# Fourier filter and cosine gate on one core: shared places for gate tiles, an earlier second batch, and unread products in two of TensorE's waits

## The chip, the cores and the metric

One core of one Trainium2 chip runs the kernel. The time is device microseconds of one execution; of the kernel before there are three runs, 2515.46, 2516.33 and 2518.54 us, median 2516.33. A profile of one further execution, taken by the hardware profiler, is read throughout.

## The reference

```python
# x: (8, 3008, 256); filters: (1505, 256); w_in: (256, 2048); w_out: (2048, 256), float32
X = np.fft.rfft(x, axis=1)
y = np.fft.irfft(X * (filt_r + 1j * filt_i)[None], n=3008, axis=1)
y = y.reshape(8 * 3008, 256)
h = y @ w_in
g = h * np.cos(h)
return g @ w_out
```

Every sequence is filtered in the frequency domain, and then each of the 24064 tokens goes through a hidden layer of 2048 with the gate h cos(h).

## The kernel before, in words

**The transforms.** 3008 is 47 x 64, so a sequence's transform is done as two short ones, written as matrix products: `stage1` (length 47; 7 pieces a batch), `stage23` (length 64, the filter, and length 64 back; 12 pieces a batch) and `stage4` (length 47 back; units of up to five short sequences, which give the columns of `y`). Between the stages the data goes through HBM: ScalarE's queue writes `z1t` and `z2t`, SyncE's queue (SP) reads `xf`, `zf`, `f` and `z` (`z4` in the code). Batch 0 has code of its own (`first1`, `first23`), whose products are plain float32; the others split each float32 number into a high and a low part (`xh`, `xl`; `zh`, `zl`; `yh`, `yl`) and add three products (`mm3`).

**The hidden layer.** The tokens come in 47 chunks of 512 (`c`), the hidden units in 8 parts of 256 (`s`), so there are 376 steps. `hidden(c, s)` makes `hp` with 12 products of 128x128 by 128x512 (L469), and `gate` turns it into `gh` and `gl`: two VectorE operations bring h into the range of the sine (L481, L482), ScalarE takes the sine (L483), VectorE multiplies by h (L484), ScalarE casts the high part `gh` (L485), and GpSimd subtracts it to leave the low part `gl` (L486). `project(c, s)` adds three products of `gh` and `gl` with `w_out` into `acc` (L497), two steps later (`LAG = 2`). After the eighth part ScalarE writes `acc` to the tile `o` (L514) and a transfer takes it out. `hp` has two places in PSUM, `acc` one for each half. So the products of step k+2 need L484 of step k to have read `hp`.

**Places.** A tile's name or tag has a number of places, and a new tile waits until an old one's last reader is done. `g`, `gh`, `gl` have two each of 4 KB a partition, `o` two of 2 KB; the transforms' results `z1t` and `z2t` share the tag `st` with four places of 2 KB.

**Order.** The 376 steps are written one behind the other, 8 slots each. A planner (`plan`, `run_due`) gives each part of a transform a due slot and hands it out between the parts of the steps, TensorE's parts at least `APART = 3` slots apart. Batch b is planned to end at slot 376 b - `BEFORE`; batch 1 gets `LATER` slots more, and starts at `FIRST`. A unit of `stage4` is handed out when all of its batch's `stage23` pieces have been written. From all this a scheduler with a timing model writes each engine's order of instructions at compile time; `tc.high_priority()` puts instructions ahead there, `tc.issue_after(i)` puts them behind `i` on its engine. At run time every engine follows its own order. The weights are split into high and low parts by `prep_w` while the first steps run (L231 to L239, on ScalarE, VectorE and GpSimd).

The places and the plan before, the lines that the change touches:

```python
LATER = 54
...
g = moe.tile([P, 2, TC], F32, name="g")
gs[c, s] = gh, gl = [moe.tile([P, 2, TC], F32R, name=v) for v in ("gh", "gl")]
...
o = moe.tile([P, TC], F32, name="o")
...
end = slot(b * S) - BEFORE
if b == 1:
    end += LATER
start = max(end - LENGTH, FIRST)
step = (end - start - GAP12) / (2 * n1 + 2 * n23)
```

## Time and profile before

| what | value |
|---|---|
| median of three runs | 2516.33 us |
| profiled execution, whole | 2517.33 us |
| its span, first to last instruction | 2515.5 us |
| mean granted TensorE clock | 0.988 |
| TensorE busy | 2454.9 us (98%) |
| VectorE busy | 1889.6 us (75%) |
| GpSimd busy | 1426.9 us (57%) |
| ScalarE busy | 1286.4 us (51%) |

Busy time is time in which an engine has an instruction under way; products overlap at their ends. PE is TensorE's products, PEld its weight loads, DVE is VectorE, ACT is ScalarE, POOL is GpSimd, SP is SyncE, and a q behind an engine's name is its queue of instructions. A row of the timeline gives the start, the length, the engine, the line of the kernel, the operation, what it writes and reads, how many instructions are merged, and in brackets how long the engine had been idle and what ended that. The granted clock is the share of full speed that TensorE's throttle allowed.

### The profile page before, as it was taken

To read this page: it belongs to the slowest core of one execution; us is meant where nothing else is said; L and a number is where in the kernel's file an instruction comes from. 1 tells how busy PE (TensorE), PEld (TensorE's weight loads), DVE (VectorE), ACT (ScalarE), POOL (GpSimd) and SP (SyncE) were. 2 spreads that over 40 slices of the span, in tenths; PEclk is the share of its full clock that TensorE was granted. 3 is DMA by queue.
4 is the path that set the end of the run, shared out by engine and by line. 5 is a ranking of instruction groups with operands and counts; after the bars stand their busy time and mean duration, and the time that the engine had idled before them with its cause. 6 is when DMAs were issued, how large, how long until landed. Compare 5 with 4: busy or idle time off the path is not lost.

```text
span 2515.5 us, 29899 instructions
## 1 busy us (share of the span) xinstructions
PE 2454.9 (98%) x10783; PEld 1967.7 (78%) x10783; DVE 1889.6 (75%) x1917; ACT 1286.4 (51%) x1709; POOL 1426.9 (57%) x825
## 2 busy tenths in 40 slices
PE   7789999999999999999999999999999999999999
PEld 2567777888888888888888888888888888888887
DVE  2697886887678876888678877788768886666666
ACT  1654555555455554555545555555555554444443
POOL 1775665656556655656556565565656654444443
PEclk8799999999999999999999999999999999999999
DMA  9633334223232221322223232222313211000000
GB/s 321 208 91 96 120 105 129 91 79 91 70 93 90 96 79 51 108 88 87 79 76 100 85 110 61 82 96 75 89 40 98 96 47 49 30 17 9 17 9 18
DMA packets 135121, 212.27 MB, mean 84 GB/s; under 512 B 12765, under 2 KB 64781, under 8 KB 134973
## 3 DMA queue, kind: packets, MB, share of 16 engines
q1 hardware_dynamic: 82577, 137.85, 18.4%
q10 hardware_dynamic: 52396, 72.50, 8.8%
q8 instruction: 86, 1.41, 0.2%
q14 instruction: 62, 0.51, 0.1%
HBM read 135.33 MB, written 74.97 MB: 84 GB/s over the span
## 4 chain that ended last, share of the span: by engine, by line
PE 85%; DVE 7%; DMA 3%; issue 2%; ACT 2%; POOL 1%; SPq 0%; ACTq 0%; DVEq 0%; POOLq 0%
PE hp L469 38%; PE acc L497 37%; PE ps L435 3%; PE ps L251 2%; PE ps L252 2%; PE ps L253 2%; DVE g L481 1%; DVE sw L325 1%; DVE g L482 1%; DVE g L484 1%; DMA xf<-in_x 1%; ACT g L483 1%; DVE xo L280 1%; DMA zf<-z 0%; PE hp L378 0%
## 5 line engine op out<-in xcount | busy, mean ns | idle before, releaser
L486 POOL TENSOR_TENSOR gl<-g,gh 128x1024 fp32r<-128x1024 f32 x375 | 908.6, 2423 | 812.8 <-ACT gh L485 490.9
L469 PE MATMUL hp<-y,w_in 128*128 128x512 f32 x4512 | 1138.8, 401 | 18.4 <-DVE g L484 15.9
L469 PEld LDWEIGHTS hp<-y,w_in 128*128 128x128 f32 x4512 | 846.2, 190 | 219.0 <-issue 9.4
L497 PE MATMUL acc<-gh,w_out 128*128 128x512 f32 x3008 | 896.2, 396 | 1.3 <-ACT gh L485 1.3
L484 DVE TENSOR_TENSOR g<-g,hp 128x1024 f32<-128x1024 f32 x377 | 458.1, 1215 | 326.6 <-ACT g L483 325.6
L483 ACT ACTIVATE g<-g,half_pi 128x1024 f32<-128x1024 f32 x377 | 433.6, 1150 | 479.9 <-DVE g L482 435.4
L497 PEld LDWEIGHTS acc<-gh,w_out 128*128 128x128 f32 x3008 | 563.1, 188 | 132.2 <-ACT gh L485 2.2
L485 ACT CAST gh<-g 128x1024 fp32r<-128x1024 f32 x377 | 395.2, 1048 | 401.5 <-DVE g L484 381.9
L481 DVE TENSOR_SCALAR g<-hp 128x1024 f32<-128x1024 f32 x377 | 458.6, 1216 | 126.3 <-PE hp L469 122.0
L497 PE MATMUL acc<-gl,w_out 128*128 128x512 f32 x1504 | 548.3, 399 | 0.1
L482 DVE SCALAR_TENSOR_TENSOR g<-g,hp 128x1024 f32<-128x1024 f32 x377 | 457.9, 1215 | 9.4
L497 PEld LDWEIGHTS acc<-gl,w_out 128*128 128x128 f32 x1504 | 282.8, 188 | 65.1 <-POOL gl L486 0.7
L435 PEld LDWEIGHTS ps<-m,z 120*128 120x128 f32 (+1 forms) x816 | 129.3, 193 | 29.2 <-DMA z<-z 7.8
L452 POOL TENSOR_TENSOR y<-y,y 128x470 fp32r<-128x470 f32 (+29 forms) x142 | 127.1, 899 | 42.9 <-ACT y L449 42.8
L331 POOL TENSOR_TENSOR yl<-ya,yh 128x512 fp32r<-128x512 f32 x84 | 111.5, 1328 | 58.2 <-ACT yh L330 55.7
L314 POOL TENSOR_TENSOR zl<-zf,zh 128x512 fp32r<-128x512 f32 x84 | 111.9, 1333 | 48.2 <-DVE zh L313 21.1
L435 PE MATMUL ps<-m,z 120*128 120x120 f32 (+1 forms) x816 | 130.4, 275 | 7.5 <-DMA z<-z 7.0
L325 DVE SCALAR_TENSOR_TENSOR sw<-sw,sg,f 128x256 f32<-128x256 f32 x168 | 116.7, 734 | 0.0
L330 ACT CAST yh<-ya 128x512 fp32r<-128x512 f32 x84 | 51.8, 618 | 115.1 <-DVE ya L327 115.1
L313 DVE CAST zh<-zf 128x512 fp32r<-128x512 f32 x84 | 86.2, 1026 | 29.8 <-DMA zf<-z 18.2
L327 DVE TENSOR_TENSOR ya<-ya,sw 128x512 f32<-128x512 f32 x84 | 100.6, 1198 | 0.1
L280 DVE TENSOR_TENSOR xo<-xf 120x512 f32<-120x512 f32 (+1 forms) x49 | 55.0, 1123 | 40.9 <-DMA xf<-in_x 40.8
(98 smaller groups left out, 1429.2 us busy)
## 6 DMA issues: line engine op xcount, KB each, us to landing
z<-z SPq DMA_DIRECT2D x101, 240.0 KB, 3.2
out_t<-o ACTq DMA_DIRECT2D x93, 256.0 KB, 2.0
f<-in_fb SPq DMA_DIRECT2D x84, 256.0 KB, 3.1
f<-in_fa SPq DMA_DIRECT2D x84, 256.0 KB, 3.4
zf<-z SPq DMA_DIRECT2D x84, 256.0 KB, 3.5
z<-z2t ACTq DMA_DIRECT2D x84, 256.0 KB, 2.0
xf<-in_x SPq DMA_DIRECT2D x42, 480.0 KB, 4.3
z<-z1t ACTq DMA_DIRECT2D x84, 240.0 KB, 2.5
```

Source lines behind the costliest of these rows:

```text
L314: nc.gpsimd.tensor_tensor(lo, zf, hi.bitcast(F32), ALU.subtract)
L325: nc.vector.scalar_tensor_tensor(sw[:, ks], sw[:, ks], sg[:, 2 * i + k : 2 * i + k + 1], fbt[:, ks], ALU.mult, ALU.mult)
L435: nc.tensor.matmul(v[:, t, a * r : (a + 1) * r], zf[:, a, t * P : (t + 1) * P], mats[f"m4{a}"][:r, :r], start=True, stop=True)
L452: (nc.vector if i < 2 * n_first else nc.gpsimd).tensor_tensor(yl, part, yh.bitcast(F32), ALU.subtract)
L469: nc.tensor.matmul(hp[:, u], w_in[s][w][:, t, fs], y[:, t], start=(t == 0 and n == 0), stop=(t == NDT - 1 and n == 2))
L481: nc.vector.tensor_scalar(g, h, 0.25, MAGIC, ALU.add, ALU.add)
L482: nc.vector.scalar_tensor_tensor(g, g, MAGIC, h, ALU.subtract, ALU.subtract)
L483: nc.scalar.activation(g, g, AF.Sin, bias=half_pi, scale=-TWO_PI)
L484: nc.vector.tensor_tensor(g, g, h, ALU.mult)
L485: nc.scalar.copy(gh, g)
L486: engine.tensor_tensor(gl, g, gh.bitcast(F32), ALU.subtract)
L497: nc.tensor.matmul(acc, w_out[s][w][:, u, es], g[:, u], start=(s == 0 and u == 0 and n == 0), stop=(s == NFT // 2 - 1 and u == 1 and n == 2))
```

## The change

Five edits. The last piece of `first23` (batch 0) gets six products that nobody reads behind its last product (`WARM4`), and step (0, 1) gets sixteen behind its last (`WARM_GATE`); both write a place of `acc`. `g` and `gl` share one tag with five places instead of two and two. `o` takes its place among the four of `st`. `LATER` is 44 instead of 54.

```diff
-LATER = 54
+LATER = 44
...
+WARM4, WARM_GATE = 6, 16
...
+    def keep_busy(after, m, data, times):
+        with tc.issue_after(after), tc.high_priority():
+            ps = ps_o.tile([P, 512], F32, name="acc0")
+            for _ in range(times):
+                nc.tensor.matmul(ps[: m.shape[1], : data.shape[1]], m, data, start=True, stop=True)
...
-            nc.tensor.matmul(ps, mats["f3i"], yb, start=False, stop=True)
+            m = nc.tensor.matmul(ps, mats["f3i"], yb, start=False, stop=True)
+            if i == n23 - 1:
+                keep_busy(m.ins, mats["f3i"], yb, WARM4)
...
-        g = moe.tile([P, 2, TC], F32, name="g")
-        gs[c, s] = gh, gl = [moe.tile([P, 2, TC], F32R, name=v) for v in ("gh", "gl")]
+        g = moe.tile([P, 2, TC], F32, name="g", tag="g", bufs=5)
+        gh = moe.tile([P, 2, TC], F32R, name="gh")
+        gl = moe.tile([P, 2, TC], F32R, name="gl", tag="g", bufs=5)
+        gs[c, s] = gh, gl
...
+        if (c, s) == (0, 1):
+            keep_busy(m.ins, w_in[s][0][:, 0, :P], yh[:, 0], WARM_GATE)
...
-                o = moe.tile([P, TC], F32, name="o")
+                o = fft.tile([P, TC], F32, name="o", tag="st", bufs=4)
```

## The prediction

> **What bounds the kernel now.** I read the busy shares first, then busy time by stretch, then TensorE's own waits, then the timeline of each stretch that loses time. The page:

> ```profile
> PE 2454.9 (98%) x10783; PEld 1967.7 (78%) x10783; DVE 1889.6 (75%) x1917; ACT 1286.4 (51%) x1709; POOL 1426.9 (57%) x825
> ```

> TensorE is busy in 2454.9 of 2515.5 us. The same by stretch:

> ```profile
> 72.00:96.00 24.00, 15.05 (x57) 12.32 (x56) 7.64 (x18) 15.55 (x33) 17.44 (x15) 0.64 0.76 254
> 96.00:120.00 24.00, 18.67 (x85) 15.57 (x85) 21.63 (x24) 16.67 (x27) 16.88 (x11) 0.86 0.74 228
> 120.00:160.00 40.00, 33.34 (x123) 25.60 (x122) 39.74 (x30) 19.77 (x30) 34.12 (x20) 0.87 0.34 91
> 160.00:235.00 75.00, 74.98 (x337) 60.56 (x337) 57.37 (x56) 37.41 (x54) 43.22 (x28) 1.00 0.33 94
> 235.00:310.00 75.00, 67.75 (x285) 53.30 (x284) 68.22 (x72) 41.82 (x58) 46.82 (x29) 0.95 0.35 112
> 380.00:410.00 30.00, 24.84 (x109) 18.44 (x108) 15.49 (x20) 15.08 (x25) 13.61 (x11) 0.94 0.51 137
> 410.00:2400.00 1990.00, 1988.50 (x8929) 1618.07 (x8928) 1521.93 (x1546) 1036.41 (x1353) 1147.22 (x659) 1.00 0.24 74
> ```

> Columns: length, busy PE, PEld, DVE, ACT, POOL, then clock, DMA share, GB/s. From 410 to 2400 us TensorE idles 1.5 us in 1990 at full clock, so nothing in the change can win there: all the gain must come from 72 to 410 us, where PE idles 9.0, 5.3, 6.7, 7.2 and 5.2 us in the quoted stretches and a few us more are lost to a low clock. At 120 to 160 VectorE is busy 39.74 of 40: there VectorE, not TensorE, is the bound. TensorE's list of waits has the gate on top:

> ```profile
> PE hp L469 <- DVE g L484: 15.9, 14, 3.4
> ```

> The first stretches in the timeline of PE, then two rows of the clock by the microsecond, then one full-speed group from the chain of waits:

> ```profile
> 71.73 1.02 PE L403 MATMUL hp<-yb,f3i 128*128 128x512 f32 x2
> 79.46 2.06 PE L435 MATMUL hp<-m,z 120*128 120x120 f32 x8 [6.71 <-DMA z<-z]
> 87.30 8.13 PE L469 MATMUL hp<-y,w_in 128*128 128x512 f32 x24 [2.24 <-ACT y L449]
> 95.27 1.05 PE L435 MATMUL ps<-m,z 120*128 120x120 f32 x8
> 101.64 1.64 PE L435 MATMUL ps<-m,z 120*128 120x120 f32 x6 [5.33 <-DMA z<-z]
> 134.15 8.56 PE L469 MATMUL hp<-y,w_in 128*128 128x512 f32 x24 [2.06 <-DVE g L484]
> 153.09 6.67 PE L469 MATMUL hp<-y,w_in 128*128 128x512 f32 x21 [3.38 <-DVE g L484]
> ```

> ```profile
> 74.00:75.00 1.00, 0.00 (x0) 1.00 0.00 0
> 76.00:77.00 1.00, 0.00 (x0) 0.50 0.02 4
> ```

> ```profile
> 442.55 2.80 PE hp L469 x12
> ```

> Twelve products at full clock take 2.80 us (0.233 each), so 24 take 5.6: the 8.13 at 87.30 holds 2.5 us of low clock, the 8.56 at 134.15 holds 3.0, the 21 at 153.09 hold 1.8. The two idle times of 6.71 and 5.33 us, both ended by the load of `z`, are "TensorE's two waits".

> **The change part by part.**

> *Six unread products ahead of the first stage-4 product (WARM4).* One such F32 product is two records that take 1.02 us, their overlapping ends included, so six take at most 6.1 us, from 72.7 to 78.8, inside a wait that a DMA ends at 79.46: on the path they cost nothing. If all ran at half clock (12.2 us) they would stick out by 5.5. What can they gain? The clock was still 1.00 two us after the last product and 0.50 at four. With the filler it stays up at 79.46, so the three stage-4 groups of about 2 us take 1 us each. But PE then idles from about 82.5 to 87.3, where ScalarE and VectorE still make `y`; that is 4.8 us, longer than the pause that dropped the clock here. So I expect the products at 87.30 to start at half clock again. [...]

> *Sixteen unread products behind step (0,1) (WARM_GATE).* 16 x 0.233 = 3.7 us from 95.3, in a pause that lasts until 101.64. Queued behind them on PE is the stage-4 group of 95.27, which then ends near 100.2 instead of 96.3. Who waits for that:

> ```profile
> 79.17 8.77 SPq L412 DMA_DIRECT2D z<-z2t  x12
> 88.73 0.58 SPq L222 DMA_DIRECT2D raw<-in_w_out  x1
> 94.40 0.67 ACT L231 ACTIVATE o<-raw 128x512 f32<-128x512 f32 x1 [1.98 <-DMA raw<-in_w_out]
> 95.17 0.43 DVE L234 TENSOR_SCALAR t<-o 128x512 int32<-128x512 int32 x1 [4.83 <-ACT o L231]
> 99.07 0.34 ACT L441 COPY odd<-ps 128x240 f32<-128x240 f32 x1
> 102.37 1.21 DVE L484 TENSOR_TENSOR g<-g,hp 128x1024 f32<-128x1024 f32 x1
> ```

> The copy `odd` slips from 99.07 by up to 1.1 us and ScalarE's next sine with it, so the gate's last step at 102.37 slips by up to about 1. The rows show something more important: the first gate follows `t` at 95.17 on VectorE, which a weight load, issued by SP at 88.73, releases. That issue stands on SP behind twelve others that fill 79.17 to 87.9, so it hangs on SP's queue and not on TensorE. So a faster TensorE before 95 us does not start VectorE's full stretch sooner, and what it wins is lost in the next gate wait. Both fillers together: between -5.9 (2.5 at 87.30, and at most 3.4 in the stretch 96 to 120, whose clock averages 0.86 over 24 us) and +8 (both at half clock: 5.5, and 7.5 us in a pause of 5.3). I take 0, by the row at 95.17, the one that releases the gates.

> *Five shared places for g and gl.* Before, g of step k waits for the place of k-2, that is for POOL's L486. Afterwards three g can be alive while two gl are. Steps (0,4) to (0,7):

> ```profile
> 136.18 5.19 POOL L486 TENSOR_TENSOR gl<-g,gh 128x1024 fp32r<-128x1024 f32 x2 [0.93 <-ACT gh L485]
> 139.04 4.58 DVE L280 TENSOR_TENSOR xo<-xf 120x512 f32<-120x512 f32 x2
> 143.54 3.49 DVE L281 TENSOR_TENSOR xf<-xf 120x512 f32<-120x512 f32 x2
> 146.96 1.21 DVE L481 TENSOR_SCALAR g<-hp 128x1024 f32<-128x1024 f32 x1
> ```

> The products of (0,6) end near 139.6, yet VectorE first does the first-stage work of batch 1 and opens that gate at 146.96; PE pays 3.38 at 153.09. The place of g(0,4) came free with the first of the two L486, near 138.8, so at run time the place did not hold the gate: the order did, and that order was written at compile time, where the place may have been the reason. Bounds: 0 (the order stays) and -10.2 (both gate waits of this stretch with their low clock: 2.06 + 3.0 + 3.38 + 1.8). I take -4: one of the two goes (5.1), less about 1, since the postponed first-stage work then stands ahead of later gates. The places of gh stay two, so nothing else in the gate gets free.

> *Outputs in the transforms' places.* The same memory: one place more of 4 KB a partition, two of 2 KB fewer. ScalarE's `o` may now wait for a transform tile that is still being written out; behind it on ScalarE stand sine and gh, and POOL and PE wait for these. The price of one such wait is at most a landing:

> ```profile
> z<-z2t ACTq DMA_DIRECT2D x84, 256.0 KB, 2.0
> ```

> With four places in turn and one transform tile in several us it is covered; from 0 to +2, taken as 0.

> *Batch 1 planned sooner (LATER 54 to 44).* Its plan ended at slot 376 - 160 + 54 = 270, now 260; the start stays 60; a step goes from 190/38 = 5.0 slots to 180/38 = 4.74. A slot is about 0.8 us ((2515.5 - 87.3) us over 3024 slots), so the end moves by 8 us. The end matters, because chunk 5 contains batch 1's first tokens:

> ```profile
> 380.34 0.35 ACTq L342 DMA_DIRECT2D z<-z2t  x1
> 382.75 1.81 SPq L425 DMA_DIRECT2D z<-z  x4
> 384.39 1.20 PE L497 MATMUL acc<-gh,w_out 128*128 128x512 f32 x4 [0.92 <-ACT gh L485]
> 387.23 2.23 PE L435 MATMUL ps<-m,z 120*128 120x120 f32 x16 [1.65 <-DMA z<-z]
> 391.77 0.46 PE L251 MATMUL ps<-xh,m1e 120*120 120x512 f32 x1 [0.44 <-DVE y L443]
> 406.05 0.36 PE L251 MATMUL ps<-xh,m1e 96*96 96x256 f32 x1 [1.82 <-ACT z1t L295]
> 407.04 4.28 PE L469 MATMUL hp<-y,w_in 128*128 128x512 f32 x12 [0.24 <-DVE g L484]
> ```

> The last write of batch 1 goes out at 380.34, four loads queue at 382.75, PE stands still. The four waits of 0.92, 1.65, 0.44 and 1.82 and the low clock at 407 (4.28 for 2.80) make 6.3 us. Eight us earlier should clear the first three and part of the rest: -4.5. Against that, more of the transforms comes into 235 to 310, where VectorE is busy 68.22 of 75 and PE already idles 7.2:

> ```profile
> L325 DVE SCALAR_TENSOR_TENSOR sw<-sw,sg,f 128x256 f32<-128x256 f32 x168 | 116.7, 734 | 0.0
> L313 DVE CAST zh<-zf 128x512 fp32r<-128x512 f32 x84 | 86.2, 1026 | 29.8 <-DMA zf<-z 18.2
> L327 DVE TENSOR_TENSOR ya<-ya,sw 128x512 f32<-128x512 f32 x84 | 100.6, 1198 | 0.1
> ```

> A second-stage piece costs VectorE at least 2 x 0.73 + 1.03 + 1.20 = 3.7 us; 5% more pieces there is about half a piece, +1.5 to +2. The moved steps' loads (SP: xf, f, zf) and writes (ScalarE's queue) move too, into a stretch with a DMA share near 0.35, so I cost them at nothing; if the loads fell into 96 to 120 (share 0.74) each would delay a weight load behind it on SP. Bounds -6.3 and +7.4 (two whole pieces). I take -3.

> Sum against the profiled execution (2517.3 us, span 2515.5): 2517.3 + 0 - 4 + 0 - 3 = 2510.3; it lies 1.0 above the median of 2516.3, so I say 2510 (a mean run would be nearer 2509).

> **The rivals.**
> *The fillers pay too (2504 to 2506).* If the compiled order puts the gates ahead of the weight preparation at 95.17, TensorE's speed counts, and up to 5.9 us come off on top of the 7: 2504. For: VectorE idles 4.83 us just there. Against: the pause from 82.5 to 87.3. [...]
> *The change moves nothing (2512 to 2520).* The order on VectorE stays as it is, or one gate wait gives way to another: the work of 120 to 160 is the same and VectorE has 0.26 us free. What LATER wins at 384 it gives back before 310. For: at run time the place was free before it was needed.
> *Slower: batch 1 crowds VectorE (2522 to 2527).* From 235 to 310 each piece of 3.7 us that stands ahead of a gate is a wait of PE. Two more pieces (7.4) and a lost clock window as at 134 (3.0), against -3 to -4 at 384 and the gates left as they are, give about +6; it decides from one and a half pieces on. For: 14 waits on the gate already. Against: from 160 to 235 VectorE has 17.6 us free, which can take early pieces.

> **How the numbers follow.** Forecast 0.42 (2506 to 2512), fillers pay 0.13, nothing 0.30, slower 0.15. About 0.2% (5 us, below 2511.3 or above 2521.4) is what a measurement here can tell from no change. Faster: nine tenths of the forecast and the fillers' case, 0.51; same: 0.30 and the rest of the forecast, 0.34; slower 0.15. The range 2501 to 2520 leaves out the slower case, and below it takes in the fillers' case with the larger ends of the other two terms in part; the forecast's own range is 2506 to 2512.

> **What the profile after would show.** PE has 10783 + 12 + 16 = 10811 products, the clock is 1.00 at 79 us, and the idle times before the stage-4 products shrink to under 2 and 3 us. Right on the places: L481 of (0,6) comes within 2 us of its products, and no gate wait above 2 us is left in 120 to 160. Right on LATER: batch 1's last write goes out near 372, and the stretch 380 to 410 idles under 2 us. The forecast is wrong if PE still idles over 6 us in 120 to 160, or if 235 to 310 idles over 10.

## The result, and the profile after

The changed kernel takes 2760.31 us (median of four, 2755.07 to 2768.52) against 2517.11 (2515.46 to 2518.54): 1.097 of the time before, 95% interval 1.094 to 1.100. The forecast was 2510. The profiled execution of after has a span of 2753.3 us, 237.8 more than before, at a mean granted clock of 0.976.

Busy time and the costliest groups on the page of after:

```profile
PE 2543.7 (92%) x10811; PEld 1980.8 (72%) x10811; DVE 1887.8 (69%) x1917; ACT 1291.3 (47%) x1709; POOL 1434.0 (52%) x825
L502 POOL TENSOR_TENSOR gl<-g,gh 128x1024 fp32r<-128x1024 f32 x375 | 905.5, 2415 | 950.2 <-ACT gh L501 924.8
L500 DVE TENSOR_TENSOR g<-g,hp 128x1024 f32<-128x1024 f32 x377 | 458.1, 1215 | 427.3 <-ACT g L499 427.3
L497 DVE TENSOR_SCALAR g<-hp 128x1024 f32<-128x1024 f32 x377 | 457.7, 1214 | 41.1 <-PE hp L483 41.0
```

The same groups of before, 16 lines higher in the code:

```profile
L484 DVE TENSOR_TENSOR g<-g,hp 128x1024 f32<-128x1024 f32 x377 | 458.1, 1215 | 326.6 <-ACT g L483 325.6
L481 DVE TENSOR_SCALAR g<-hp 128x1024 f32<-128x1024 f32 x377 | 458.6, 1216 | 126.3 <-PE hp L469 122.0
L486 POOL TENSOR_TENSOR gl<-g,gh 128x1024 fp32r<-128x1024 f32 x375 | 908.6, 2423 | 812.8 <-ACT gh L485 490.9
```

No operation of the gate became slower: counts and mean durations of its steps are those of before, and VectorE, ScalarE and GpSimd are busy within 8 us of what they were. The waits moved. Before, the gate's first step waited for products (122.0 us): TensorE set the pace. After, it hardly does (41.0), and the steps inside the gate wait longer for one another: the pace is set by the gates. By stretch, after:

```profile
72.00:96.00 24.00, 19.45 (x70) 14.14 (x69) 10.14 (x20) 16.38 (x33) 17.77 (x14) 0.79 0.80 264
96.00:120.00 24.00, 22.37 (x113) 18.24 (x111) 21.47 (x28) 17.28 (x30) 21.05 (x14) 1.00 0.85 239
120.00:160.00 40.00, 32.65 (x133) 23.98 (x133) 34.92 (x31) 19.97 (x26) 32.51 (x18) 1.00 0.27 73
160.00:235.00 75.00, 64.24 (x282) 51.02 (x281) 59.05 (x62) 38.48 (x62) 46.60 (x31) 0.95 0.45 135
235.00:310.00 75.00, 67.97 (x281) 52.70 (x280) 54.33 (x55) 37.58 (x52) 42.26 (x24) 0.95 0.30 98
380.00:410.00 30.00, 28.60 (x130) 22.70 (x129) 19.60 (x20) 13.69 (x21) 17.22 (x12) 1.00 0.26 66
410.00:2400.00 1990.00, 1854.23 (x7956) 1457.63 (x7955) 1394.22 (x1412) 945.68 (x1246) 1045.97 (x605) 0.98 0.24 72
```

Up to 160 us nothing is lost: 72 to 96 holds 70 products instead of 57, but 21 of them are unread ones, and 96 to 120 holds 113 instead of 85, nine of them unread. The loss lies in what follows, from 160 us on, above all in the long middle: 410 to 2400 holds 7956 products where it held 8929, and TensorE idles 135.8 us there instead of 1.5. The missing 973 products would have taken about 217 us at the 0.223 us that one took there before; some 134 us of that is idle time, and the rest goes because a product took 0.233 us on average, beside a granted clock of 0.98 instead of 1.00. TensorE's largest wait, and two of VectorE's, in after's lists of waits:

```profile
PE hp L483 <- DVE g L500: 120.2, 77, 5.0
```

```profile
DVE g L500 <- ACT g L499: 427.3, 282, 6.0
DVE y L453 <- ACT odd L452: 103.1, 34, 5.1
```

One place of the middle shows how a gate gets long. VectorE and ScalarE in the timeline of after:

```profile
889.39 1.22 DVE L498 SCALAR_TENSOR_TENSOR g<-g,hp 128x1024 f32<-128x1024 f32 x1
894.19 0.41 DVE L453 TENSOR_TENSOR y<-ps,odd 128x240 f32<-128x240 f32 x1 [3.58 <-ACT odd L452]
...
896.31 1.31 DVE L334 SCALAR_TENSOR_TENSOR sw<-sw,sg,f 128x256 f32<-128x256 f32 x2
897.54 1.21 DVE L500 TENSOR_TENSOR g<-g,hp 128x1024 f32<-128x1024 f32 x1
```

```profile
889.17 0.60 ACT L530 ACTIVATE o<-acc 128x512 f32<-128x512 f32 x1 [2.21 <-PE acc L513]
...
891.69 1.07 ACT L501 CAST gh<-g 128x1024 fp32r<-128x1024 f32 x1
...
893.79 0.36 ACT L452 COPY odd<-ps 128x240 f32<-128x240 f32 x1 [1.03 <-PE ps L446]
894.50 0.58 ACT L328 COPY sw<-ps 64x512 f32<-64x512 f32 x1 [0.34 <-PE ps L254]
895.09 0.58 ACT L329 COPY sw<-ps 64x512 f32<-64x512 f32 x1
895.70 1.16 ACT L499 ACTIVATE g<-g,half_pi 128x1024 f32<-128x1024 f32 x1
```

The sine's argument is ready at 890.6. From then on ScalarE's order still has the second copy of `o`, two of `z2t`, a cast, and the copies of `odd` and `sw` (which wait 1.03 and 0.34 us for transform products) ahead of the sine, which starts at 895.70. L500 follows at 897.54, behind VectorE's work on `sw`: 8.15 us after L498 began. Before, at about the same time, VectorE needed 2.51 us from L482 to L484:

```profile
891.60 1.22 DVE L482 SCALAR_TENSOR_TENSOR g<-g,hp 128x1024 f32<-128x1024 f32 x1
894.11 1.22 DVE L484 TENSOR_TENSOR g<-g,hp 128x1024 f32<-128x1024 f32 x1 [1.28 <-ACT g L483]
```

Over the steps that lie between 70 and 330 of the 376, the trace gives a step of 6.35 us before and 7.06 after, a gate (L481 to the start of the subtraction) of 7.0 and 8.4, and a pause between the end of the products and L481 of 0.83 and 3.39. Most of what the gate grew by is spent waiting for ScalarE to come to it: 0.75 us more before the sine and 0.50 more before the cast. 0.71 us in each of 376 steps are 267 us, somewhat more than the 238 seen over the whole.

### The profile page after: what moved, and what is told of

Read it like the earlier page. It is cut to its first block, busy times and chain, and to the rows that moved or that the text cites. A ratio compares the mean times of both kernels' runs of the same rounds, so it can differ in the third digit from the quotient of the medians.

```text
span 2753.3 us, 29437 instructions
## 1 busy us (share of the span) xinstructions
PE 2543.7 (92%) x10811; PEld 1980.8 (72%) x10811; DVE 1887.8 (69%) x1917; ACT 1291.3 (47%) x1709; POOL 1434.0 (52%) x825
## 4 chain that ended last, share of the span: by engine, by line
PE 57%; DVE 17%; DMA 8%; ACT 6%; POOL 5%; issue 5%; SPq 0%; ACTq 0%; POOLq 0%; DVEq 0%
PE hp L483 28%; PE acc L513 24%; DMA xf<-in_x 4%; DVE sw L334 4%; DVE g L500 3%; DVE g L498 3%; POOL gl L502 3%; ACT g L499 2%; DVE g L497 2%; PE ps L446 2%; POOL xl L296 2%; DMA zf<-z 1%; DVE xo L289 1%; DVE ya L331 1%; ACT gh L501 1%
## 5 line engine op out<-in xcount | busy, mean ns | idle before, releaser
L483 PE MATMUL hp<-y,w_in 128*128 128x512 f32 x4512 | 1166.2, 409 | 123.9 <-DVE g L500 120.2
L483 PEld LDWEIGHTS hp<-y,w_in 128*128 128x128 f32 x4512 | 866.4, 195 | 371.4 <-issue 92.5
L500 DVE TENSOR_TENSOR g<-g,hp 128x1024 f32<-128x1024 f32 x377 | 458.1, 1215 | 427.3 <-ACT g L499 427.3
L497 DVE TENSOR_SCALAR g<-hp 128x1024 f32<-128x1024 f32 x377 | 457.7, 1214 | 41.1 <-PE hp L483 41.0
L498 DVE SCALAR_TENSOR_TENSOR g<-g,hp 128x1024 f32<-128x1024 f32 x377 | 458.0, 1215 | 10.1
L334 DVE SCALAR_TENSOR_TENSOR sw<-sw,sg,f 128x256 f32<-128x256 f32 x168 | 161.9, 1001 | 0.0
L460 ACT CAST y<-y 128x470 fp32r<-128x470 f32 (+29 forms) x150 | 68.0, 458 | 187.0 <-PE hp L483 140.7
L453 DVE TENSOR_TENSOR y<-ps,odd 128x240 f32<-128x240 f32 (+1 forms) x102 | 40.8, 400 | 151.7 <-ACT odd L452 102.6
L446 PEld LDWEIGHTS ps<-m,z 120*128 120x128 f32 (+1 forms) x816 | 107.8, 195 | 21.6 <-DVE ya L331 5.0
L446 PE MATMUL ps<-m,z 120*128 120x120 f32 (+1 forms) x816 | 110.5, 279 | 8.6 <-DVE ya L331 3.1
L322 DVE CAST zh<-zf 128x512 fp32r<-128x512 f32 x84 | 70.1, 836 | 70.4 <-PE ps L253 42.8
L530 ACT ACTIVATE o<-acc 128x512 f32<-128x512 f32 x94 | 55.9, 597 | 130.3 <-PE acc L513 130.3
## 6 DMA issues: line engine op xcount, KB each, us to landing
out_t<-o ACTq DMA_DIRECT2D x93, 256.0 KB, 2.0
f<-in_fb SPq DMA_DIRECT2D x84, 256.0 KB, 3.1
f<-in_fa SPq DMA_DIRECT2D x84, 256.0 KB, 3.4
zf<-z SPq DMA_DIRECT2D x84, 256.0 KB, 2.8
z<-z2t ACTq DMA_DIRECT2D x84, 256.0 KB, 2.4
```

What stands on the lines that cost most here:

```text
L334: nc.vector.scalar_tensor_tensor(sw[:, ks], sw[:, ks], sg[:, 2 * i + k : 2 * i + k + 1], fbt[:, ks], ALU.mult, ALU.mult)
L446: nc.tensor.matmul(v[:, t, a * r : (a + 1) * r], zf[:, a, t * P : (t + 1) * P], mats[f"m4{a}"][:r, :r], start=True, stop=True)
L483: m = nc.tensor.matmul(hp[:, u], w_in[s][w][:, t, fs], y[:, t], start=(t == 0 and n == 0), stop=(t == NDT - 1 and n == 2))
L497: nc.vector.tensor_scalar(g, h, 0.25, MAGIC, ALU.add, ALU.add)
L498: nc.vector.scalar_tensor_tensor(g, g, MAGIC, h, ALU.subtract, ALU.subtract)
L500: nc.vector.tensor_tensor(g, g, h, ALU.mult)
```

## The experiments

Theories, as they came: the sharing of places is at fault, through the order that it makes the scheduler write; or the number of places, the outputs in `st`, the fillers or `LATER` are; later, that the order harms because transform products are bunched between the hidden products. Medians are set against runs of the kernel before on the same chip (2515.63, 2516.82, 2516.9 and 2517.4 us in the four sets).

**The places undone, and alone.** e1 is after with one edit undone:

```diff
-        g = moe.tile([P, 2, TC], F32, name="g", tag="g", bufs=5)
-        gh = moe.tile([P, 2, TC], F32R, name="gh")
-        gl = moe.tile([P, 2, TC], F32R, name="gl", tag="g", bufs=5)
-        gs[c, s] = gh, gl
+        g = moe.tile([P, 2, TC], F32, name="g")
+        gs[c, s] = gh, gl = [moe.tile([P, 2, TC], F32R, name=v) for v in ("gh", "gl")]
```

> The changed kernel with one edit undone: g and gl have two places each of their own again; fillers, outputs in st and LATER 44 stay. Order theory (sharing one tag makes the compile-time order bunch the transforms): 2500 to 2518 us, transforms spread over the steps, TensorE idle below 70 us in all. Output theory (o in the transforms' places blocks ScalarE at each chunk's end): still 2740 to 2780, since o stays in st. Planner theory (LATER 44 or the fillers upset the plan): still above 2700.

Measured: 2508.71 us, 0.9975 [0.9966, 0.9985]. e2 is before with one edit made, the four places merely put together:

```diff
-        g = moe.tile([P, 2, TC], F32, name="g")
+        g = moe.tile([P, 2, TC], F32, name="g", tag="g", bufs=4)
...
+        gl = moe.tile([P, 2, TC], F32R, name="gl", tag="g", bufs=4)
```

> The kernel before with one edit: g and gl share four places instead of two and two; o, LATER 54 as before, no fillers, the same memory. Order theory: slow, 2680 to 2800, bunched. Output theory: 2512 to 2522, o has its own places. A theory that only the fifth place or the mixture of edits does it: 2512 to 2522.

Measured: 2738.18 us, 1.0882 [1.0864, 1.0900]. Its waits have the same head as after's:

```profile
PE hp L471 <- DVE g L486: 113.1, 76, 5.8
```

So the loss belongs to `g` and `gl` under one tag. No memory is lacking: four are as many as two and two. Nor is a place taken over from another tile than before: in the compiled program of e2, as in that of before, `g` of step k stands where `g` of step k-2 stood, and `gl` where `gl` of k-2 stood, in every step from 10 to 369. What differs is the order of instructions. After, too, had no wait for a place where a gate begins. In its trace VectorE's idle time before L497 ends with the products of `hidden` and with nothing else (61 times, 41.0 us):

```profile
L497 DVE TENSOR_SCALAR g<-hp x377: 684/1217/1226, 91.7 to 2744.0; 128x1024 f32<-128x1024 f32 x188, 128x512 f32<-128x512 f32 x1
...
  PE hp L483: 41.0, 61
```

**The same places, another order of statements.** e3 keeps all edits and states the subtraction of step k only behind the first VectorE operation of gate k+1. e4 does the same to e2.

```diff
+    def low():
+        if lows:
+            gl, g, gh = lows.pop()
+            nc.gpsimd.tensor_tensor(gl, g, gh.bitcast(F32), ALU.subtract)
...
+        low()      # behind the gate's first operation
...
-        engine.tensor_tensor(gl, g, gh.bitcast(F32), ALU.subtract)
+        lows.append((gl, g, gh))      # GpSimd's only
```

> The changed kernel, all five edits, but the code states the subtraction gl of step k only behind the first gate operation of step k+1; places, operations and counts are the same. Order theory (places of one tag are handed out in the order of their first writers, so g of k+1 had to wait for gl of k): even order, 2500 to 2520. Run-time theory (g must wait on the chip until project three steps back has read its gl): places are the same, so still 2740 to 2780.

> The kernel before with four shared places, and the subtraction gl stated one gate later. Order theory: 2505 to 2525. Run-time theory: as slow as with four shared places and the old statement, above 2680.

Measured: e3 2498.87 us, 0.9936 [0.9921, 0.9951], the shortest of all and below both kernels; e4 2503.71, 0.9952 [0.9937, 0.9967]. Both lie some 1 us below the ranges given to the theory of the order, and far below those of the run-time theory. The same stretches and wait in e3:

```profile
96.00:120.00 24.00, 24.00 (x121) 20.06 (x120) 21.75 (x24) 18.76 (x30) 19.98 (x13) 1.00 0.82 239
120.00:160.00 40.00, 32.74 (x132) 25.16 (x131) 36.38 (x36) 20.49 (x29) 34.58 (x20) 0.96 0.33 85
310.00:380.00 70.00, 66.03 (x285) 53.07 (x284) 50.88 (x56) 39.03 (x57) 45.44 (x28) 0.95 0.40 114
410.00:2400.00 1990.00, 1989.46 (x8930) 1619.57 (x8930) 1523.85 (x1547) 1038.10 (x1353) 1140.43 (x658) 1.00 0.24 73
```

```profile
PE hp L483 <- DVE g L508: 10.1, 5, 3.8
```

The middle is whole again, 8930 products, and the gate wait is 10.1 us. The number of places, the operations and their counts are those of after, so neither sharing nor the number of places costs the time; the order in which the first writers of `g` and `gl` are stated does. (Which tile a place is taken over from does change from after to e3; that this isn't it follows from e2 and from the waits at L497.)

What the compiled orders of instructions add: in before the next gate's L481 stands ahead of this gate's L484 on VectorE in 15 of 376 steps, in e1 in 15, in e3 in 10; in after, e2 and g1 (below) in none. With the late statement and no sharing, each engine's compiled order is that of before, line for line. Asking for the next `g` tile one step sooner in the code leaves the order of after unchanged. (These two were compiled only, not run.) The reading, which is inferred: places of a tag are handed out in the order in which their first writers are stated, so `g` of step k+1 comes behind `gl` of step k, whose first writer is the gate's last operation. In the scheduler's timeline the gates then form a chain and bound the plan, and every engine's order is written for a slower step. On the chip nothing holds the next gate that long: in the trace of after its L497 starts, on average, 1.3 us before this gate's subtraction.

**Own places, three and two; the fillers; LATER.** f3 is after with

```diff
-        g = moe.tile([P, 2, TC], F32, name="g", tag="g", bufs=5)
+        g = moe.tile([P, 2, TC], F32, name="g", bufs=3)
...
-        gl = moe.tile([P, 2, TC], F32R, name="gl", tag="g", bufs=5)
+        gl = moe.tile([P, 2, TC], F32R, name="gl", bufs=2)
```

f4 is e3 without its two calls of `keep_busy`; f1 is before with these two calls alone, f2 before with `LATER = 44` alone.

> All edits, but the five places are three for g and two for gl, under names of their own. Order theory: even order, 2497 to 2508; about 2499 if the places themselves are what brought the run with the later statement below the one without sharing. Theory that the fifth place harms at run time: above 2520.

> The five edits with the later statement of gl, without the unread products. If the fillers pay: 2502 to 2506, about 4 us more than with them (2499). If they are worth nothing: 2497 to 2500.

> The kernel before with the twenty-two unread products (WARM4 and WARM_GATE) alone. As predicted (VectorE's first gate hangs on a weight load, so a faster TensorE before 95 us is worth nothing): 2513 to 2518. If TensorE's clock and head start count there: 2509 to 2512, as the first 160 us of the run without sharing suggest (some 17 products ahead at 160 us).

> The kernel before with LATER 44 alone. As predicted: 3 us less, 2510 to 2515, with the waits of 380 to 410 us gone and a little more idle time in 235 to 310. Rival: VectorE is crowded, 2517 to 2522.

Measured: f3 2499.29 us, 0.9930 [0.9916, 0.9943], as good as e3; f4 2507.10, 0.9963 [0.9950, 0.9975]; f1 2505.35, 0.9954 [0.9942, 0.9967]; f2 2508.64, 0.9969 [0.9958, 0.9980]. So a third place for `g` is what the five places were good for, and it needs no sharing. The edits don't add up: fillers alone -11.5 and `LATER` alone -8.2, but all but the places (e1) only -6.9, and in e3 the fillers are worth about 7 (0.9963 without them, 0.9936 with them). f1 and f2 came out below both of the ranges that I had given them, and f4 1 us above the nearer of its two. f2 by stretch, and then one row of before:

```profile
235.00:310.00 75.00, 73.88 (x327) 59.61 (x327) 68.65 (x73) 43.67 (x61) 51.06 (x30) 1.00 0.33 108
310.00:380.00 70.00, 65.02 (x284) 51.30 (x283) 56.57 (x57) 40.19 (x56) 43.13 (x25) 1.00 0.39 120
380.00:410.00 30.00, 26.13 (x118) 21.07 (x117) 15.41 (x21) 15.06 (x26) 14.15 (x12) 0.89 0.44 117
```

```profile
310.00:380.00 70.00, 67.85 (x293) 53.60 (x292) 62.20 (x58) 39.29 (x56) 44.31 (x26) 1.00 0.35 105
```

It gains in 235 to 310 (idle 1.1 us, before 7.2), and hardly in 380 to 410 (3.9, before 5.2); in 310 to 380 it loses some of that again (5.0, before 2.1).

**Is it bunching?** In the trace of before 12% of the steps 40 to 340 have no transform product behind their hidden products, in after 57%, and there the transforms are crowded into three of the eight steps of a chunk. g1 is after with each of TensorE's transform parts tied behind the hidden product where the planner put it; h1 adds the same to e3.

```diff
+            with tc.issue_after(mm[0]) if pe and mm else nullcontext():
+                next(g, None)
-            next(g, None)
```

> The changed kernel, places shared and gl stated as in it, but each TensorE part of a transform is tied behind the hidden product in front of which the planner put it, so it cannot be ordered earlier. No gate begins before the one before it has ended (as in the changed kernel), yet the transforms are spread over the steps. Bunching theory (the time is lost because transforms crowd into three of eight steps): 2495 to 2525. Gate theory (the time is lost because the gates follow one another): 2700 or more.

> The tie of g1_held (each TensorE part of a transform behind the hidden product that the planner put it behind) together with the later statement of gl. If the tie itself cost the time in g1_held: 2700 or more again. If the hand-out of places does (g of the next step waits for the place of this step's gl): 2495 to 2530.

Measured: g1 2792.74 us, 1.1089 [1.1074, 1.1104]; h1 2510.37, 0.9973 [0.9963, 0.9983]. In g1 the transforms are spread again (12% of the steps have none), and it is the slowest of all. Its waits:

```profile
PE hp L483 <- DVE g L501: 178.9, 131, 5.0
```

```profile
DVE g L501 <- ACT g L500: 433.5, 285, 6.3
DVE ya L331 <- ACT sw L329: 95.0, 56, 5.0
```

h1 shows that where gates may overlap the tie by itself costs some 9 us (0.9973 against 0.9936 for e3), not 240. The bunching theory falls: spreading the transforms doesn't help, and what is left is the way in which the places are handed out. (ScalarE's waits for `acc` ahead of the copies of `o` also grew in after, from 28.5 to 130.3 us; I take them for another symptom, which no run tests by itself.)

**The small edits one by one.** g2 is before with the six unread products alone, g3 with the sixteen alone, g4 with `o` in `st` alone.

```diff
+                keep_busy(m.ins, mats["f3i"], yb, WARM4)                             # g2
+            keep_busy(m.ins, w_in[s][0][:, 0, :P], yh[:, 0], WARM_GATE)              # g3
-                o = moe.tile([P, TC], F32, name="o")
+                o = fft.tile([P, TC], F32, name="o", tag="st", bufs=4)               # g4
```

> The kernel before with the six unread products alone. If the second pause before the first step closes the clock again, as predicted: 2514 to 2518. If they make most of the fillers' gain of 11: 2506 to 2510.

> The kernel before with the sixteen unread products alone. If the gain is theirs: 2506 to 2510; if not: 2514 to 2518. The two shares should add up to about 11 if they work independently.

> The kernel before with the outputs in st alone. As predicted: no difference, 2515 to 2519. If ScalarE waits there for transfers: up to 2525.

Measured: g2 2503.13 us, 0.9942 [0.9929, 0.9954]; g3 2511.02, 0.9973 [0.9963, 0.9984]; g4 2516.06, 0.9997 [0.9988, 1.0006]. I had expected the six and the sixteen to add up to about 11; alone they bring 13.8 and 5.9, together (f1) 11.5. TensorE and VectorE in g2:

```profile
79.73 1.15 PE L446 MATMUL hp<-m,z 120*128 120x120 f32 x8 [2.10 <-DMA z<-z]
87.20 8.15 PE L480 MATMUL hp<-y,w_in 128*128 128x512 f32 x24 [4.24 <-ACT y L460]
```

```profile
92.83 1.22 DVE L492 TENSOR_SCALAR g<-hp 128x1024 f32<-128x1024 f32 x1 [2.58 <-PE hp L480]
95.22 0.42 DVE L235 TENSOR_SCALAR t<-o 128x512 int32<-128x512 int32 x1
```

The 24 products at 87.20 still take 8.15 us (before 8.13): the clock fell again in the second pause, from 1.00 at 84 to 85 us over 0.73 to 0.50 at 86 to 87. Yet the edit alone brings 13.8 us. With it the scheduler writes the first gate (92.83) ahead of the weight preparation (95.22), as in f1, e1 and e3, which also have the six products; in before, f2, f4 and g3, which don't, it stands behind. That this one change of order makes the whole gain isn't shown.

**Which sharing?** h2 lets `g` and `gh` share five places, h3 `gh` and `gl`; the third tile keeps two of its own.

```diff
-        gh = moe.tile([P, 2, TC], F32R, name="gh")
-        gl = moe.tile([P, 2, TC], F32R, name="gl", tag="g", bufs=5)
+        gh = moe.tile([P, 2, TC], F32R, name="gh", tag="g", bufs=5)                  # h2
+        gl = moe.tile([P, 2, TC], F32R, name="gl", bufs=2)                           # h2
-        g = moe.tile([P, 2, TC], F32, name="g", tag="g", bufs=5)
+        g = moe.tile([P, 2, TC], F32, name="g", bufs=2)                              # h3
+        gh = moe.tile([P, 2, TC], F32R, name="gh", tag="gx", bufs=5)                 # h3
+        gl = moe.tile([P, 2, TC], F32R, name="gl", tag="gx", bufs=5)                 # h3
```

> The changed kernel, but g shares its five places with gh, and gl has two of its own. The next gate's g then has to wait only for this step's gh, one operation behind L484, and in the compile-time order no gate begins before the one before it has ended, as in the slow kernels, though the transforms are spread. If gates that never overlap are enough to lose the time: 2700 or more. If it is the wait up to gl, some 2 us later: 2495 to 2530.

> The changed kernel, but gh and gl share five places and g has two of its own. Sharing as such, or the release of a place by another engine at run time, would cost here too: above 2600. If only a g that stands behind a gl in the hand-out costs: 2495 to 2510.

Measured: h2 2502.71 us, 0.9939 [0.9925, 0.9954]; h3 2504.17, 0.9948 [0.9933, 0.9963]. Sharing as such costs nothing. h2 limits my reading: there too no L481 stands ahead of the L484 of the gate before, and the kernel is fast. So it isn't the overlap of gates that is needed. By my reading it matters how far into the gate the plan holds the next one: up to the cast on ScalarE (h2) or up to the subtraction on GpSimd (after).

## Why the prediction was wrong, point by point

**The step that failed** is "Five shared places for g and gl", taken as -4 us with bounds 0 and -10.2. Alone (with four places) it costs 222.6 us (e2: 2738.18 against 2515.63), and without it the other edits give 2508.71 (e1), less than before. So it is the whole loss of 243.2, and more. I had weighed only when a place comes free at run time ("near 138.8") and had noticed that "the order did, and that order was written at compile time"; but I asked of the new places only what order they would free, never what order they impose. By the reading above a shared tag is also a queue: its places are handed out in one order for both names. That made a loss possible, and nothing in the trace of before excluded it, so a bound of 0 on that side had no row behind it.

**"Nothing in the change can win there"** (410 to 2400) was right, and hid the risk: where TensorE idles 1.5 us of 1990 a change can still lose, and 973 products fewer were done there.

**What the step hoped for exists.** With the order repaired, the third `g` brings 2508.71 to 2498.87 (e1 to e3), 9.8 us, near the larger end. It isn't where I put it: the gate waits of 120 to 160 stay (5.0 us in e3, 5.4 before), and L481 of (0,6), which was to come within 2 us of its products, comes 7.3 us behind them in e3 as in before, and 7.0 in after. That the number fits the larger end is luck. The sign of being wrong that I had set for this stretch, over 6 us of idle time, appeared (7.4 us in after, 7.3 in e3); the one for 235 to 310, over 10, did not (7.0 in after). e1 had in the stretches of 120 and of 310 us:

```profile
120.00:160.00 40.00, 31.04 (x120) 23.46 (x119) 39.57 (x30) 17.43 (x25) 33.92 (x19) 0.91 0.34 85
310.00:380.00 70.00, 61.98 (x264) 48.97 (x264) 49.59 (x53) 37.48 (x54) 42.07 (x24) 0.98 0.38 113
```

Against e3's 132 and 285 products, most of the gain lies in these two.

**The fillers, taken as 0.** The count of 10811 came as told, and the first wait shrank to 2.1 us (I had said under 2). That the six hold the clock up to the second pause came true in g2, where the clock is 1.00 up to 85 us and the stage-4 groups from 79.73 on take 1.15, 1.15 and 1.07 us, but not in after. There the clock gave way 0.5 us into them, and they take 1.68, 1.91 and 1.90:

```profile
79.00:80.00 1.00, 0.70 (x5) 0.87 1.13 159
80.00:81.00 1.00, 1.00 (x7) 0.50 0.70 230
```

```profile
79.30 1.68 PE L446 MATMUL hp<-m,z 120*128 120x120 f32 x8 [2.09 <-DMA z<-z]
80.77 1.91 PE L446 MATMUL ps<-m,z 120*128 120x120 f32 x8
82.62 1.90 PE L446 MATMUL hp<-m,z 24*128 24x24 f32 x8
```

The size failed too: -11.5 together, beyond the bound of -5.9. The condition of my rival "the fillers pay too" came true (the gate ahead of the weight preparation), but not its mechanism: in g2 TensorE is no faster at 87.20. I had taken the order at 95.17 as given while adding instructions from which the scheduler makes it. On the clock, g2's pause of 4.24 us before 87.20 cost full speed, but so did pauses of 2.09 us in after (the rows above) and of 2.06 before 134.15 in before (0.64 at 133 to 134 us, then 0.50). And in before the row of 75 to 76 us (clock 0.63) puts the fall some 2.5 us after the last product's end:

```profile
75.00:76.00 1.00, 0.00 (x0) 0.63 0.27 61
```

g2's pause of 2.10 us before 79.73, as long as after's, cost nothing: the clock is 1.00 there. So the length of a pause, from which I had argued, doesn't by itself tell whether the clock falls.

**Outputs, taken as 0:** 0.9997 alone, right. **LATER, taken as -3:** -8.2 alone, the sign right and the size past the bound of -6.3. Batch 1's last write goes out where I put it, near 372 (before 380.34), as the timeline of f2 shows:

```profile
371.67 0.33 ACTq L351 DMA_DIRECT2D z<-z2t  x1
```

But 380 to 410 still idles 3.9 us there, not under 2: the wait for `z` is gone, and a gate wait of 3.2 us stands in its place. I had feared a crowd in 235 to 310, and the gain lay there: my slower rival pointed at the stretch that improved most.

**The rivals.** None foresaw it: all priced single waits of some us in the first 410 us. The slower one, +6, was on the right side by another mechanism and a fortieth of the size.

**Open.** The rule by which places are handed out is inferred from compiled orders and from e1 to e4, h2 and h3. The traces put most of the gate's growth before the sine and the cast on ScalarE, but which single positions in the orders cost most wasn't separated by a run; nor why the edits' gains don't add up.

## What to carry to other kernels

Before two names share a tag, write down who writes each tile first and in which order these writers are stated. If places are handed out as the runs here suggest, the next round's first tile gets its place behind this round's last, and where that is the last step of a chain, the chain is laid end to end in the plan. If one role lacks places, give them to it under a name of its own (three and two were as fast here as five shared with the statement moved). Where a scheduler writes the order, every edit may change it everywhere: the long stretch that cannot win can still lose.

## What the runs showed of the hardware that I had not expected

VectorE, ScalarE and GpSimd worked within 8 us of what they did before (1887.8, 1291.3 and 1434.0 us against 1889.6, 1286.4 and 1426.9), and still 10% of time went. At 47% busy ScalarE still held the gates up: in the place shown above a sine whose argument was ready at 890.6 us stood behind copies that waited 1.03 and 0.34 us for products, and started at 895.70. TensorE's clock was lower too: over 410 to 2400 us the granted clock is 0.98 in after where it was 1.00, beside waits for the gate of up to 5.0 us.
